# Seven instead of six quads of weights prepared in the fourth block, 3.3 chunks apart

## The chip, the cores and the metric

One core of a Trainium2 chip runs the whole program. The metric is the device time of one execution in microseconds. The kernel before took 774.9 us (median of three runs, 772.95 to 774.94).

## The reference

Attention with a band mask (four heads of 32 keys, four of every fourth key among 128), then two feed-forward layers on 2304 tokens of 512 features, all in float32; the weights are given as float64 words.

```python
x = attention(q, k, v)                     # (2304, 512)
h = x @ w_in; x = (h * cos(h)) @ w_out     # first feed-forward, width 2048
h = max(max(x @ w1, x @ w2), x @ w3)       # second feed-forward, width 768
out = h @ w_out2
```

## The kernel before

**Precision.** Every float32 operand of the large products is split into a high half (a cast) and a low half (the operand less its high half), and a product is three TensorE passes: high by high, low by high, high by low. So each operand costs one cast (ScalarE, VectorE or GpSimd) and one subtraction (VectorE or GpSimd).

**Stages.** Tokens of the first feed-forward go in five blocks: four of 512 and one of 256 tokens. A block is 16 steps, one for each 128 columns of the inner width; steps are numbered through, so the fourth block is steps 48 to 63 and the fifth 64 to 79. A step `s` has eight chunks of three matmuls: four of the first layer for step `s` (line 452, 512 or 256 columns), and four of the second layer for step `s - 3` (line 551). Between the two lie the argument reduction (`ff1_reduce`, lines 519 to 531), the sine on ScalarE (line 534), the product (line 540), its high half (line 541, which is recorded as line 214 on ScalarE and line 210 on GpSimd, in turn in the fourth block) and its low half (line 542). The halves `gt` have two buffers, so the high half of step `s` waits until TensorE has finished the second layer of step `s - 2`, at the end of step `s + 1`. Attention of later blocks runs beside the steps; its last pair is in the fourth block.

**The second feed-forward's weights.** They are multiplied by a seven-product scheme for 2 by 2 quarters. The weights come in nine quads of 2 by 2 quarter blocks; each quad needs four sums of quarters and the high and low halves of seven operands. The quads lie in DRAM as `wd`, and the finished halves are kept in DRAM as `opd`.

- Quads in `PRE` (2 to 7) are prepared in the fourth block: `pre_load` (line 708) loads the quad's two raw tiles `rawp`, from a pool of three buffers that the attention's `e` tiles use too; `pre_part` (line 714) makes one of four pieces. Pieces 0 and 1 are two sums (line 729, VectorE), a cast (line 735, ScalarE) and a subtraction (line 736, VectorE); pieces 2 and 3 a cast and a subtraction on GpSimd. Each piece takes its tiles from the five buffers of tag `qkv`, and stores its two halves to `opd` (line 740). The code writes a quad over two steps, one piece at chunks 2 and 6 of each, beginning at step 51; the next quad's load follows piece 3.
- Quads 0, 1 and 8 are prepared later: `raw_load` (line 644), `a_sums` (line 654, sums on line 667) and `a_part` (line 671, a cast on ScalarE, line 638, and a subtraction on GpSimd, line 639), with `a_keep` (line 701) to store them. `ff2_early` (line 975) does this for quads 0 and 1 in the fifth block, beside the making of the second layer's inputs from `x1raw` (`b_load`, line 800, five buffers of tag `qkv`; `b_make`, line 807).
- For every other quad, and for all of them in the second and third pass over tokens, `a_part` loads `wa` from `opd` (line 693).

**What sets the order.** TensorE's instructions are kept in the order of the code. From the fourth block on the order of the other engines and of SyncE's queue is chosen by the tile framework: the place in the code is a preference, an instruction can be put earlier or later, and each engine then works in the chosen order and waits at an instruction whose inputs aren't there.

```python
made = q < NQUAD and q not in PRE          # a_part, line 675
...
x = a1 if n == 2 else a22                  # pre_part, line 731
hl = [place(name, F32R)[:, :cols] for name in ("hi", "lo")]
nc.scalar.copy(hl[0], x)
(nc.vector if n < 2 else nc.gpsimd).tensor_tensor(
    out=hl[1], in0=x, in1=hl[0].bitcast(F32), op=ALU.subtract)
```

Of the kernel before, what the change touches and what calls it, by code (L numbers as in the profile page):

```python
# [30 lines left out]
NF1 = FF1 // 128  # L31
# [9 lines left out]
NB2 = NT // (2 * HALF)  # L41
NQUAD = 3 * NF2 // 2
LAG = 3
PRE = range(2, 8)
RUNS = 5
KEYS = 2 * QB + WIN
WSLOTS = 2 * NF1
# [117 lines left out]
def body(  # L165
# [381 lines left out]
    def acc_chunk(t0, first, last, w, gt, dm, copied=True):  # L547
        n_tok = gt.shape[-1]
        a_dm = acc[dm][:, :n_tok]
        for n, (a, x) in enumerate(PASSES):  # L550
            pe(nc.tensor.matmul(  # L551
                a_dm,
                w[:, a, 128 * dm : 128 * dm + 128],
                gt[:, x, :],
                start=first and n == 0,
                stop=last and n == 2,
            ))
        if last and copied:
            acc_copy(t0, n_tok, dm, "V" if dm % 2 else "A")
# [19 lines left out]
    def raw_exponent(n):  # L579
        if 0 <= n < len(halves2):  # L580
            exponent(pieces2[n])
# [47 lines left out]
    def slot_tile(n, shape, dt, name):  # L629
        return wp.tile(shape, dt, tag=f"w{n}", name=name)  # L630
# [13 lines left out]
    def raw_load(q):  # L644
        if q < NQUAD and q not in PRE:
            raws[q] = slot_tile(q % 3, [128, 2, 512], F32, "raw")
            nc.sync.dma_start(out=raws[q], in_=wd[q])
# [6 lines left out]
    def a_sums(q, n):  # L654
        if q < NQUAD and q not in PRE:
            r = raws[q]
            a11, a12, a21, a22 = (r[:, i, 256 * k : 256 * k + 256] for i in range(2) for k in range(2))
            if n == 0:
                if q < 2:
                    sums[q] = slot_tile(9, [128, 4, 256], F32, "ws")  # L660
                else:
                    sums[q] = gp.tile([128, 4, 256], F32, tag="g", name="ws")
                do = ((0, a21, a22, ALU.add), (1, sums[q][:, 0], a11, ALU.subtract))
            else:
                do = ((2, a11, a21, ALU.subtract), (3, a12, sums[q][:, 1], ALU.subtract))
            for k, x, y, op in do:
                nc.vector.tensor_tensor(out=sums[q][:, k], in0=x, in1=y, op=op)
# [3 lines left out]
    def a_part(q, n):  # L671
        if q >= NB2 * NQUAD:
            return
        cols = 256 * len(PARTS[n])
        made = q < NQUAD and q not in PRE
        dt = F32R if made else F32
# [21 lines left out]
    def kept_at(q, n):  # L698
        return opd[q, :, 2 * n : 2 * n + len(PARTS[n])].rearrange("p a n -> p (a n)").rearrange("p (a n) -> p a n", a=2)
# [8 lines left out]
    def pre_load(q):  # L708
        if q in PRE:
            raw_pre[q] = [sp.tile([128, 512], F32, tag="e", name="rawp") for _ in range(2)]  # L710
            for i in range(2):
                nc.sync.dma_start(out=raw_pre[q][i], in_=wd[q, :, i])

    def pre_part(q, n):
        if q not in PRE:
            return
        a1, a2 = raw_pre[q]
        a11, a12, a21, a22 = (r[:, 256 * k : 256 * k + 256] for r in (a1, a2) for k in range(2))
        place = lambda name, dt: ip.tile([128, 512], dt, tag="qkv", name=name)
        if n < 2:  # L720
            x = place("ws", F32)
            x1, x2 = x[:, :256], x[:, 256:]
            if n == 0:
                raw_pre["s2"] = x2
                do = ((x1, a21, a22, ALU.add), (x2, x1, a11, ALU.subtract))
            else:
                do = ((x1, a11, a21, ALU.subtract), (x2, a12, raw_pre.pop("s2"), ALU.subtract))
            for out, i0, i1, op in do:
                nc.vector.tensor_tensor(out=out, in0=i0, in1=i1, op=op)
        else:  # L730
            x = a1 if n == 2 else a22
        cols = x.shape[-1]
        part = (1, 2, 0, 3)[n]
# [3 lines that stand above are left out]
            out=hl[1], in0=x, in1=hl[0].bitcast(F32), op=ALU.subtract  # L737
        )
        for k in range(2):
            nc.sync.dma_start(out=kept_at(q, part)[:, k], in_=hl[k].bitcast(F32))  # L740
# [333 lines left out]
    def weight_loads(n, upto):  # L1074
        for _ in range(n):
            if at[0] < upto:
                w_load(order[at[0]], src[order[at[0]]])
                at[0] += 1
# [39 lines left out]
    def h_of(s):  # L1118
        t, f = divmod(s, NF1)
        if t < NBT - 1:  # L1120
            hv = (bank[6] if s == 2 else h_bank[(s + (s > 2)) % 2])[:, : BLOCKS[t]]
        else:
            hv = bank[4 + (s + 2) % 4][:, : BLOCKS[t]]
        return hv, h_chunks(hv, halves[("in", f)], STARTS[t] % RING, BLOCKS[t])
# [4 lines left out]
    n = len(first)  # L1129
# [172 lines left out]

    in_order = {e.engine for e in (nc.tensor, nc.vector, nc.scalar, nc.gpsimd)}
    NS = NBT * NF1
    PRE_AT = NS - 2 * NF1 + 3
    for s in range(NS + LAG):
        phase[0] = 1 if s < NF1 else 2 if s < NS - NF1 else 3
        assert s % NF1 or finished >= set(sum(plan[: s // NF1 + 1], []))
        if s == 0:
            weight_loads(WSLOTS, WSLOTS)  # L1310
        if s == PINNED:
            fixed.append(len(nc.cur_bb.bb.instructions))
        chunks = []
        if s < NS:
            hv, hc = hs[s] = hs[s] if s in hs else h_of(s)
            chunks += [("h", n, c) for n, c in enumerate(H_ORDER) if n >= begun.get(s, 0)]
        if s >= LAG:
            chunks += [("a", dm, 0) for dm in range(NC)]
        if NF1 <= s < PINNED:

            def chunk1(kind, x, c):
                if kind == "h":
                    hc(x, c)
                else:
                    t0, f0 = divmod(s - LAG, NF1)
                    last = f0 == NF1 - 1
                    acc_chunk(STARTS[t0], f0 == 0, last, halves[("out", f0)], g[s - LAG], x, False)
                    if last:
                        acc_done.append((STARTS[t0], BLOCKS[t0], x))

            step1(s, [lambda c=c: chunk1(*c) for c in chunks])
            chunks = []
            pairs = [x for x in pairs if x[2] not in pairs1[: next_of.get("W", 0)]]
            continue
        events = []
        if s == NF1:
            events += [(0, lambda: ff1_high(s - 2)), (0, lambda: ff1_low(s - 2))]
        if s < NF1:

            def chunk(kind, x, c):  # L1340
                if kind == "h":
                    hc(x, c)
                else:
                    f0 = s - LAG
                    acc_chunk(0, f0 == 0, False, halves[("out", f0)], g[f0], x)

            step0(s, [lambda c=c: chunk(*c) for c in chunks])
            raw_bits(s - NF1)
            chunks = []
        for j, (kind, x, c) in enumerate(chunks):  # L1350
            upto = j if j + 1 < len(chunks) else 7
            if kind == "h":
                hc(x, c)
                if x == NC - 1 and s >= NF1:
                    ff1_reduce(s, hv)
            else:
                t0, f0 = divmod(s - LAG, NF1)
                acc_chunk(STARTS[t0], f0 == 0, f0 == NF1 - 1, halves[("out", f0)], g[s - LAG], x)
            while events and events[0][0] <= upto and not (pairs and pairs[0][0] <= 8 * s + min(events[0][0], upto)):
                events.pop(0)[1]()  # L1360
            while pairs and pairs[0][0] <= 8 * s + upto:
                att_pair(*pairs.pop(0)[1:])
                while events and events[0][0] <= upto and not (pairs and pairs[0][0] <= 8 * s + min(events[0][0], upto)):
                    events.pop(0)[1]()
            if j == 1 and s >= NF1:
                if s - 1 < NS:
                    ff1_g(s - 1)
            q, n = divmod(s - PRE_AT, 2)
            q += PRE.start
            if s == PRE_AT - 1 and j == 6:  # L1370
                pre_load(q + 1)
            if s >= PRE_AT and q in PRE and j in (2, 6):
                pre_part(q, 2 * n + j // 6)
                if n and j == 6:
                    pre_load(q + 1)
            if j == 1:
                raw_exponent(s - NF1)
            if j == 5:
                raw_bits(s - NF1)
        k = s - (NS - NF1)  # L1380
        if k >= -1:
            ff2_early(k)
# [94 lines left out]
```

## Time and profile before

| | us |
|---|---|
| median of three runs | 774.9 |
| lowest, highest | 772.95, 774.94 |
| the profiled execution | 773.13 |
| its span, first to last instruction | 771.4 |
| TensorE matmul busy | 760.3 (99%) |
| VectorE busy | 567.7 (74%) |
| ScalarE busy | 445.2 (58%) |
| GpSimd busy | 102.3 (13%) |

A busy share is an average over the whole span. The profile has further views: windows (busy time of each engine in a stretch), the timeline of one engine (start, duration, and in brackets the idle time before an instruction and what ended it), and the DMA issues with the time from issue to landing.

### The profile page before, as it was taken

The page shows a single profiled execution, that of the slowest core. Times are in us where ns is not written, and L with a number is a line of the kernel's source. Part 1 is how long each engine was busy: PE and PEld are TensorE (multiplying, and loading weights), DVE is VectorE, ACT ScalarE, POOL GpSimd, SP SyncE. Part 2 cuts the span into 40 slices and gives each one's busy share as a digit, 9 for nine tenths or more (in the row PEclk, how much of TensorE's full clock was granted, in tenths as well). Part 3 has the DMA queues.
Part 4 walks back from the last instruction along what each step waited for, and adds up shares of the span by engine and source line. Part 5 has one row for each costly group of instructions (what it writes and reads, how often), then busy time and mean ns, then how long its engine had stood idle before and what let it go on. Part 6 is the DMA issues. An engine that isn't in the chain of part 4 may idle for free.

```text
span 771.4 us, 13658 instructions
## 1 busy us (share of the span) xinstructions
PE 760.3 (99%) x4760; PEld 672.7 (87%) x4760; DVE 567.7 (74%) x1497; ACT 445.2 (58%) x1080; POOL 102.3 (13%) x107
## 2 busy tenths in 40 slices
PE   9999999999999999999999999999999999999997
PEld 7777777878878878887888899899999999999997
DVE  6999999777776788877866769996675666646742
ACT  7889999779573777764544435554434333433330
POOL 2422121302022202010112203100200000000000
PEclk9999999999999999999999999999999999999999
DMA  9983111243434443433456563398765888467802
GB/s 355 416 315 143 37 43 67 85 165 105 125 119 138 129 157 125 131 100 110 165 191 218 188 206 134 112 300 277 244 198 186 243 253 258 136 190 243 255 22 83
DMA packets 60405, 134.32 MB, mean 174 GB/s; under 512 B 6704, under 2 KB 21168, under 8 KB 60336
## 3 DMA queue, kind: packets, MB, share of 16 engines
q1 hardware_dynamic: 60336, 133.44, 51.7%
q8 instruction: 38, 0.62, 0.3%
q14 instruction: 31, 0.25, 0.1%
HBM read 101.17 MB, written 32.24 MB: 173 GB/s over the span
## 4 chain that ended last, share of the span: by engine, by line
PE 79%; DVE 10%; ACT 6%; DMA 3%; issue 1%; POOL 0%; ACTq 0%; DVEq 0%; SPq 0%
PE bank L826 25%; PE bank L551 19%; PE bank L452 19%; PE bank L944 9%; PE bank L341 2%; ACT e L291 2%; PE bank L410 2%; PE bank L393 1%; DMA wod<-wh 1%; PE bank L321 1%; ACT L291 1%; DVE ring L639 1%; DVE wx L263 1%; ACT r L291 1%; DMA wh<-in_w_o 1%
## 5 line engine op out<-in xcount | busy, mean ns | idle before, releaser
L452 PE MATMUL bank<-ring,w 128*128 128x512 f32 (+1 forms) x960 | 219.1, 374 | 1.5 <-DVE ring L434 1.5
L551 PE MATMUL bank<-gt,w 128*128 128x512 f32 (+1 forms) x960 | 215.8, 371 | 1.5 <-DVE gt L542 1.3
L826 PE MATMUL bank<-ring,wa 128*128 128x384 f32 x1134 | 198.0, 334 | 0.0
L826 PEld LDWEIGHTS bank<-ring,wa 128*128 128x128 f32 x1134 | 196.6, 188 | 0.0
L551 PEld LDWEIGHTS bank<-gt,w 128*128 128x128 f32 x960 | 166.6, 189 | 33.1 <-DVE gt L542 1.8
L452 PEld LDWEIGHTS bank<-ring,w 128*128 128x128 f32 x960 | 165.4, 189 | 34.0 <-DVE ring L434 1.9
L291 ACT ACTIVATE r<-r,hpi 128x512 f32<-128x512 f32 (+1 forms) x80 | 54.6, 683 | 54.2 <-DVE r L531 35.0
L291 ACT ACTIVATE e<-e,m 96x128 f32<-96x128 f32 x192 | 75.0, 393 | 5.8 <-DVE m L351 5.5
L842 ACT COPY s<-bank 128x384 f32<-128x384 f32 x54 | 26.0, 481 | 45.5 <-PE bank L826 45.4
L291 ACT ACT_TABLE_LOAD x38 | 48.8, 1283 | 1.7 <-PEq L1463 0.7
L351 DVE CUSTOM_DVE_ANT_0 e<-bank,cs 96x128 f32<-96x128 f32 x192 | 42.7, 282 | 9.1 <-PE bank L341 9.1
L860 DVE TENSOR_TENSOR s<-s,bank 128x384 f32<-128x384 f32 x36 | 19.9, 553 | 37.9 <-PE bank L826 37.9
L944 PE MATMUL bank<-whole,w 128*128 128x384 f32 x252 | 47.5, 334 | 0.0
L944 PEld LDWEIGHTS bank<-whole,w 128*128 128x128 f32 x252 | 44.0, 188 | 0.0
L210 POOL TENSOR_SCALAR gt<-r 128x512 fp32r<-128x512 f32 x27 | 18.9, 700 | 178.3 <-PE bank L551 120.0
L282 POOL TENSOR_TENSOR w<-wx,w 128x512 fp32r<-128x512 f32 x20 | 26.3, 1318 | 80.5 <-DVE w L214 46.5
L291 ACT ACTIVATION_READ_ACCUMULATOR e<-e,m 96x1 f32 x192 | 36.5, 190 | 0.0
L255 ACT ACTIVATE wh<-wh 128x256 f32<-128x256 f32 x48 | 20.6, 436 | 27.0 <-DMA wh<-in_w 19.2
L488 DVE CUSTOM_DVE_ANT_0 r<-bank,r 128x512 f32<-128x512 f32 x39 | 26.8, 687 | 12.8 <-ACT r L466 12.8
L496 DVE TENSOR_TENSOR r<-bank,r 128x512 f32<-128x512 f32 x47 | 32.2, 685 | 3.3 <-ACT r L291 3.1
L790 ACT CAST whole<-mx 128x384 fp32r<-128x384 f32 x36 | 18.6, 516 | 27.1 <-DVE mx L862 14.6
L385 DVE TENSOR_TENSOR e<-e,z 96x512 f32<-96x512 f32 x47 | 32.0, 710 | 0.9
(106 smaller groups left out, 992.2 us busy)
## 6 DMA issues: line engine op xcount, KB each, us to landing
wa<-opd SPq DMA_DIRECT2D x72, 512.0 KB, 4.6
qkv<-in_qkv SPq DMA_DIRECT2D x48, 336.0 KB, 4.0
wh<-in_w SPq DMA_DIRECT2D x36, 256.0 KB, 2.9
w<-in_w_in SPq DMA_DIRECT2D x16, 512.0 KB, 8.7
w<-in_w_out SPq DMA_DIRECT2D x16, 512.0 KB, 9.4
wa<-opd SPq DMA_DIRECT2D x24, 256.0 KB, 4.2
wd<-wh SPq DMA_DIRECT2D x36, 128.0 KB, 1.8
opd<-hi SPq DMA_DIRECT2D x18, 256.0 KB, 2.0
```

What stands on the lines that cost most here:

```text
L255: nc.scalar.activation(high, high, AF.Prelu, scale=2.0**-112, alpha=2.0**32)
L282: eng.tensor_tensor(out=w[:, 1, :], in0=words.pop(key), in1=w[:, 0, :].bitcast(F32), op=ALU.subtract)
L291: last_table.append(nc.scalar.activation(*args, **kw).ins)
L351: nc.vector.tensor_tensor_reduce(out=e[:, 2 * j + h, :], in0=places_of[j, h], in1=mask[:, kind, :], scale=-1.0 / math.sqrt(D), scalar=3e38 ...
L385: eng.tensor_tensor(out=e, in0=e, in1=z[:, n, :].unsqueeze(2).to_broadcast([QB, 4, KB]), op=ALU.mult)
L452: pe(nc.tensor.matmul(hv, w[:, a, 128 * c : 128 * c + 128], ring[c][:, x, c0 : c0 + n_tok], start=n == 0 and j == 0, stop=n == NC - 1 and ...
L488: nc.vector._custom_dve(dve_ops.TENSOR_ADD_SAT, out=r, in0=hv, in1=r, s0=ARG_HI, s1=ARG_LO)
L496: nc.vector.tensor_tensor(out=r, in0=hv, in1=r, op=ALU.mult)
L551: pe(nc.tensor.matmul(a_dm, w[:, a, 128 * dm : 128 * dm + 128], gt[:, x, :], start=first and n == 0, stop=last and n == 2,))
L826: nc.tensor.matmul(out, ops[q][a][:, x, 128 * c : 128 * c + 128], b_op(b, c)[:, y], start=first and c == 0 and n == 0, stop=c == 1 and n == 2,
L842: nc.scalar.copy(x, bank_of(q)[to][:, :HALF])
L944: nc.tensor.matmul(to, w[p][:, 128 * at : 128 * at + 128], x[y], start=first and k == 0 and j == 0, stop=k == len(steps) - 1 and j == 2, s ...
```

## The change

`PRE` becomes quads 1 to 7, so quad 1 is prepared in the fourth block, and the fifth loads its finished halves from `opd`. The places of the pieces are no longer chunks 2 and 6 of each step: piece `n` of the 28 stands `24 + round(3.3 n)` chunks after the beginning of the fourth block, that is from chunk 0 of step 51 to chunk 1 of step 62. The first load stands four chunks ahead of the first piece, at chunk 4 of step 50 in place of chunk 6.

```diff
-PRE = range(2, 8)
+PRE = range(1, 8)
+PRE_SLOTS = [24 + round(3.3 * n) for n in range(28)]
...
-    PRE_AT = NS - 2 * NF1 + 3
+    pre_slots = [8 * (NS - 2 * NF1) + n for n in PRE_SLOTS]
...
-            q, n = divmod(s - PRE_AT, 2)
-            q += PRE.start
-            if s == PRE_AT - 1 and j == 6:
-                pre_load(q + 1)
-            if s >= PRE_AT and q in PRE and j in (2, 6):
-                pre_part(q, 2 * n + j // 6)
-                if n and j == 6:
-                    pre_load(q + 1)
+            if 8 * s + j == pre_slots[0] - 4:
+                pre_load(PRE.start)
+            if 8 * s + j in pre_slots:
+                q, n = divmod(pre_slots.index(8 * s + j), 4)
+                pre_part(PRE.start + q, n)
+                if n == 3:
+                    pre_load(PRE.start + q + 1)
```

## Rows read from the trace of the kernel before

**Rows 1.** The page's busy times (share of the span, instructions).

```profile
PE 760.3 (99%) x4760; PEld 672.7 (87%) x4760; DVE 567.7 (74%) x1497; ACT 445.2 (58%) x1080; POOL 102.3 (13%) x107
```

**Rows 2.** Timeline of TensorE, fourth and fifth block: start, duration, what, idle before.

```profile
374.03 3.01 PE L452 MATMUL bank<-ring,w 128*128 128x512 f32 x12
...
442.40 2.88 PE L551 MATMUL bank<-gt,w 128*128 128x512 f32 x12
...
446.56 2.91 PE L551 MATMUL bank<-gt,w 128*128 128x512 f32 x12
...
450.74 2.91 PE L551 MATMUL bank<-gt,w 128*128 128x512 f32 x12
...
454.92 2.91 PE L551 MATMUL bank<-gt,w 128*128 128x512 f32 x12
...
495.85 1.84 PE L551 MATMUL bank<-gt,w 128*128 128x256 f32 x12 [0.36 <-DVE gt L542]
498.61 1.44 PE L551 MATMUL bank<-gt,w 128*128 128x256 f32 x10 [0.92 <-DVE gt L542]
500.31 1.92 PE L551 MATMUL bank<-gt,w 128*128 128x256 f32 x12 [0.26 <-ACT gt L214]
502.06 18.19 PE L826 MATMUL bank<-ring,wa 128*128 128x384 f32 x104
```

**Rows 3.** Windows: length, PE, PEld, DVE, ACT, POOL busy, clock, DMA share, GB/s.

```profile
395.90:406.80 10.90, 10.90 (x49) 9.01 (x48) 7.39 (x14) 5.12 (x9) 2.14 (x4) 1.00 0.59 210
...
475.00:483.60 8.60, 8.60 (x74) 8.60 (x74) 8.60 (x22) 5.21 (x12) 3.40 (x4) 1.00 0.37 147
```

**Rows 4.** Timeline of VectorE in the fourth block.

```profile
376.86 0.42 DVE L729 TENSOR_TENSOR ws<-rawp 128x256 f32<-128x256 f32 x1
...
400.51 0.43 DVE L729 TENSOR_TENSOR ws<-rawp 128x256 f32<-128x256 f32 x1 [2.86 <-issue]
...
401.31 0.68 DVE L526 CUSTOM_DVE_ANT_0 r<-bank,r 128x512 f32<-128x512 f32 x1
402.08 0.76 DVE L736 TENSOR_TENSOR lo<-ws,hi 128x512 fp32r<-128x512 f32 x1
...
404.63 0.68 DVE L736 TENSOR_TENSOR lo<-ws,hi 128x512 fp32r<-128x512 f32 x1
...
412.31 0.43 DVE L729 TENSOR_TENSOR ws<-rawp 128x256 f32<-128x256 f32 x1 [3.11 <-issue]
...
435.92 0.42 DVE L729 TENSOR_TENSOR ws<-rawp 128x256 f32<-128x256 f32 x1 [2.80 <-DMA rawp<-wd]
...
439.37 0.69 DVE L542 TENSOR_TENSOR gt<-r,gt 128x512 fp32r<-128x512 f32 x1
...
443.87 0.68 DVE L542 TENSOR_TENSOR gt<-r,gt 128x512 fp32r<-128x512 f32 x1
```

**Rows 5.** Timelines of GpSimd and of SyncE's queue between quads 4 and 5.

```profile
405.53 2.17 POOL L736 TENSOR_TENSOR lo<-rawp,hi 128x512 fp32r<-128x512 f32 x2 [3.23 <-ACT hi L735]
...
408.43 0.99 SPq L712 DMA_DIRECT2D rawp<-wd  x2
```

**Rows 6.** DMA issues, 374 to 450 us: count, size, median us from issue to landing.

```profile
rawp<-wd SPq DMA_DIRECT2D x9, 256.0 KB, 3.5
```

**Rows 7.** The page's DMA issues: loads of finished halves.

```profile
wa<-opd SPq DMA_DIRECT2D x72, 512.0 KB, 4.6
```

**Rows 8.** Timelines of VectorE, GpSimd and SyncE in the fifth block.

```profile
470.63 0.56 DVE L639 TENSOR_TENSOR ring<-x1raw,ring 128x384 fp32r<-128x384 f32 x1
...
477.08 1.32 DVE L542 TENSOR_TENSOR gt<-r,gt 128x256 fp32r<-128x256 f32 x1
...
480.46 0.42 DVE L667 TENSOR_TENSOR ws<-ws,raw 128x256 f32<-128x256 f32 x1
...
476.82 1.30 POOL L639 TENSOR_TENSOR wa<-raw,wa 128x512 fp32r<-128x512 f32 x1 [1.70 <-ACT wa L638]
...
443.60 2.32 SPq L804 DMA_DIRECT2D x1raw<-x1d  x5
```

## The prediction

> **What bounds the kernel now.** I read the page's busy times first. TensorE is busy for 760.3 us, 99% of the span of 771.4 us [rows 1], and the granted clock is 1.00, the 2.4 GHz level, in the windows of both blocks [rows 3]. So a change pays only where TensorE waits, and costs only where it makes TensorE wait. Next I read TensorE's own timeline through the two blocks that the diff touches [rows 2]. The reader should see three things there. From 374.03 us (first-layer matmuls of step 51) to 442.40 us (second-layer matmuls of step 63, half a step after its start) lie 12.5 steps of 5.47 us, no idle time noted, a chunk of three matmuls taking 0.68 us. At the end of the fifth block TensorE waits three times, 0.36, 0.92 and 0.26 us, all for the halves of `g`: 1.54 us together. From 502.06 us it runs on. **1.54 us, 0.2% of the time, is all that the touched stages can give back.**
>
> Then the windows by engine [rows 3]: in 475.0 to 483.6 us VectorE is busy for all 8.60 us, so there it is VectorE that falls behind and later makes TensorE wait. In 395.9 to 406.8 us, in the fourth block, it is busy for 7.39 of 10.90 us. That is the room into which the change moves work.
>
> Last, VectorE's order in the fourth block [rows 4]. The first sum of quad 2 starts at 376.86 us, that of quad 4 at 400.51, of quad 5 at 412.31, of quad 7 at 435.92: (435.92 - 376.86) / 5 = 11.81 us a quad, where the code asks for two steps, 10.94 us. Each quad starts 0.87 us later against TensorE than the one before it. The timeline puts 3.11 us of VectorE idle time ahead of 412.31. **The six quads already run as a chain of waits, not at their written places.**
>
> **The chain of one quad.** From the first sum at 400.51 to the second low half's end, 404.63 + 0.68 = 405.31 us, VectorE works without a pause, with operations of the first feed-forward between; four sums of 0.43 and two low halves of 0.68 to 0.76 us are 3.1 us of it [rows 4]. GpSimd's two low halves follow, 405.53 + 2.17 = 407.70 us [rows 5]. Behind the last store, SyncE starts the next raw loads at 408.43 us, two in 0.99 us [rows 5]. Such a load lands 3.5 us after issue in the median [rows 6], and the next quad starts at 412.31. So 4.8 us for VectorE, 2.4 for GpSimd, 0.7 for SyncE, 3.9 for the loads: 11.8 us. Nothing in the diff shortens the last three. Only the operations between can change, since the places in the code decide what is preferred. These places bind only loosely: the low half at 402.08 us stands after the clip at 401.31, though the code writes it ahead [rows 4].
>
> The Trainium skill (DMA: Bandwidth & Descriptors, Anatomy of one DMA) fits a transfer, there one that GpSimd starts, as about 2.0 us plus its bytes at 436 GB/s; I estimate 2.6 us from it for 256 KB, which would take 0.9 us off the chain and nearly close the drift of 0.87. The trace has 3.5 us, so the row holds here.
>
> **The change part by part.**
>
> Quad 1 leaves the fifth block. Four sums go there, each moving the next VectorE operation by 0.34 us (480.46 to the next one's start in the same dense stretch; take its own 0.42 us as the upper end) [rows 8]: 1.4 to 1.7 us. Its four GpSimd subtractions leave too. While one runs, at 476.82 us, a VectorE subtraction of the 256-column kind takes 1.32 instead of some 0.42 us [rows 8]; 0 to 0.9 us each, I take 0.4, four times: 1.6 us. ScalarE's four copies leave, on an engine with room. So VectorE gets about 3 us back (1.4 to 5.3), ahead of waits of 1.54 us that it causes. I book the full **-1.54 us**; the ends are 0 (the backlog of the seventh quad, below, eats it) and -1.54, since there is no more to take.
>
> In their place quad 1's operands are loaded: three loads of 512 KB and one of 256 KB, a further 1.8 MB, less the raw load of 512 KB that now goes to the fourth block. A 512 KB load takes 4.6 us from issue to landing [rows 7], and the DMA engines are 37% busy in 475.0 to 483.6 us [rows 3]. They are written three steps and more ahead of 502.06, and the operands are first used behind it. Cost 0; if a slot came free too late, one landing, 4.6 us, on the first use at 502.06 us or behind.
>
> The fourth block gets a quad: four sums, two low halves on VectorE, four copies on ScalarE, two low halves on GpSimd, two loads and eight stores on SyncE. As busy time it is hidden: VectorE has 10.90 - 7.39 = 3.51 us free in two steps [rows 3]. What counts is the chain: seven links of 11.8 us in place of six. Behind a waiting sum, VectorE's queue holds the products and low halves of `g`, and TensorE waits for those. The low half at 439.37 us ends at 440.05; TensorE uses it in step 63 at 442.40: a slack of 2.35 us. The next, 443.87 + 0.68 = 444.55 us, is used at 446.56: 2.0 us [rows 2, 4].
>
> Quad 1 can't start much ahead of where quad 2 starts now, for its second raw tile takes a buffer of the last attention pair in either kernel, so the seventh quad takes a link more: its sum at 435.92 + 11.81 = 447.7 us, the low half behind it done at 440.05 + 11.81 = 451.9. It is needed at 450.74, as a step of the fifth block is shorter: **1.1 us late**. The one after that, 444.55 + 11.81 = 456.4 us, is needed at 454.92, pushed to 456.0 by then: **0.3 us more** [rows 2, 4]. So +1.4 us at the seam. Below, the bound is 0: 1.4 us less of chain, two chunks' earlier start, and it's gone. Above, case C.
>
> SyncE's loads of the fifth block's inputs start at 443.60 us now, because their five buffers come free there [rows 8]. With seven quads they come a link later, 455.4 us, and land in some 4 us; the first split made of them starts at 470.63 [rows 8]. Cost 0, with 11 us of cover.
>
> Spacing 3.3 in place of 4 chunks: 13.2 chunks a quad, 9.0 us by the code. The chain needs 11.8, so pieces are late wherever they are written. I take 0 for it, the ends -1.4 us (sums get ahead of first-layer work, the chain shortens) and case C's price.
>
> The sum: -1.54 + 1.4 = -0.1 us with the chain as it is, -1.5 if it tightens by a quarter of a microsecond a link. I take -0.4. The profiled execution took 773.13 us, 1.7 over its span, and 1.8 below the median of 774.9 of the three runs shown; they range from 772.95 to 774.94, so either is usual. From the middle, 774.0: **773.6 us**. A measurement can tell about 0.3%, 2.3 us, from no change.
>
> **The rivals.**
>
> A, the forecast: the seventh quad hangs over the seam, costs what the end of the fifth block gives back, -0.4 us: 772.7 us from the profiled execution, 774.5 from the median. Chance 0.46.
>
> B: the pieces, written earlier, are preferred over first-layer work and a link falls below 11.6 us. No wait at the seam, all of 1.54 us is gained: 771.6 from the profiled execution, 773.4 from the median. For it: 1.7 us of the 4.8 that a link spends on VectorE aren't the quad's own work [rows 4]. Against: the other 7.0 us of a link are untouched. Chance 0.24; still within 0.3%, as a rule.
>
> C, the one that makes it slower: VectorE's queue follows the written places, 9.0 us a quad, while loads still come at 11.8. Place: quad 7's first sum is written at step 60, chunk 7, on TensorE's clock 374.03 + 9 x 5.47 + 4.8 = 428.1 us; the chain brings it at 376.86 - 1.4 + 6 x 11.81 = 446.3. Behind it stand step 60's product and halves, 2.7 us by operations of 0.43 to 0.76 us, with the two sums ahead, done at 449.0, needed at 442.40 [rows 2, 4]: TensorE waits for 6.6 us. Less 1.54: +5.1, 778.2 us from the profiled execution, 780.0 from the median. It decides from a link of 10.7 us (6 x 10.7 = 64.2 in place of 70.9). For it: the six quads now all start at the same place of the code, ahead of the same clip. Against: that they start late by now, and still don't hold TensorE up. Chance 0.21.
>
> D: more is gained than the profile shows, as executions at 774.9 us may hold longer waits of just these kinds, up to 1.8 us, that the change removes as well: 771.4 us or less, -0.45%. Chance 0.06. E: the quad is made early but something else of the fifth block's end stays late, or quad 1 isn't read from the early result: no change, 774.0. Chance 0.03.
>
> **How the numbers follow.** Slower by over 0.3%: most of C, 0.18, and 0.03 of A: 0.21. Faster by over 0.3%: D and a little of B, 0.08. Within: 0.71. The range reaches from B's and D's lower end, 771.3, into C, to 778.2.
>
> **What would show it.** Right: seven starts of quads 11 to 12 us apart in VectorE's timeline, the last near 447 us; new TensorE waits of about a microsecond at 446 to 456 us for low halves of `g`; no such waits at 495 to 501 us; TensorE dense behind. B: starts under 11.6 us apart, no wait at the seam. C: several microseconds of TensorE waits between 430 and 450 us with VectorE waiting for raw loads. The forecast is wrong if TensorE's idle time in the two blocks changes by more than 2.3 us either way, or if time moves behind 502 us.

## The result and the profile after

The changed kernel takes 779.09 us (median of four runs, 778.46 to 779.33) beside 774.31 us before (772.95 to 774.94): ratio 1.0054, 95% interval 1.0029 to 1.0079. The medians differ by 4.8 us, and the time lies just beyond the upper end of the range forecast (778.2). The profiled execution has a span of 777.3 us, 5.9 over that of before.

The page's busy times, to be set beside [rows 1]: TensorE is busy 3.1 us longer for the same 4760 matmuls, and its span grows by 5.9.

```profile
PE 763.4 (98%) x4760; PEld 673.4 (87%) x4760; DVE 567.2 (73%) x1499; ACT 443.5 (57%) x1080; POOL 99.6 (13%) x105
```

TensorE's timeline, the lines that answer to [rows 2] and those with idle time (start, duration, what, idle before and what ended it):

```profile
374.01 3.01 PE L453 MATMUL bank<-ring,w 128*128 128x512 f32 x12
...
441.68 3.02 PE L453 MATMUL bank<-ring,w 128*128 128x512 f32 x12 [1.86 <-DVE r L541]
...
447.26 1.60 PE L453 MATMUL bank<-ring,w 128*128 128x256 f32 x12
...
461.57 1.33 PE L552 MATMUL bank<-gt,w 128*128 128x256 f32 x9 [0.18 <-ACT o L565]
463.55 0.62 PE L552 MATMUL bank<-gt,w 128*128 128x256 f32 x3 [0.64 <-DVE o L565]
464.00 1.59 PE L453 MATMUL bank<-ring,w 128*128 128x256 f32 x12
...
469.46 1.45 PE L552 MATMUL bank<-gt,w 128*128 128x256 f32 x10 [0.75 <-DVE gt L543]
...
501.62 1.83 PE L552 MATMUL bank<-gt,w 128*128 128x256 f32 x12 [0.34 <-DVE gt L543]
504.38 1.45 PE L552 MATMUL bank<-gt,w 128*128 128x256 f32 x10 [0.93 <-DVE gt L543]
506.08 1.91 PE L552 MATMUL bank<-gt,w 128*128 128x256 f32 x12 [0.25 <-ACT gt L215]
507.82 2.42 PE L827 MATMUL bank<-ring,wa 128*128 128x384 f32 x13
```

Both traces have step 51's first layer at 374.0 us. From there to the first matmul of the second feed-forward it is 128.03 us before [rows 2] and 507.82 - 374.01 = 133.81 here: **5.78 of the 5.9 us lie in this stretch.** Three pieces make it up. Step 64 begins at 447.26, 73.25 us in, where before it was 71.09 (445.12 in its timeline): +2.16, with the wait of 1.86 us at 441.68. Step 68 begins at 464.00, 89.99 us in, where before it was 86.51 (460.54): another +1.32, with the waits for output copies. The other +2.30 comes behind that, a wait of 0.75 us and short gaps up to some 487 us. And the three waits at the end, which were to be gained, are still there: 1.52 us.

VectorE's timeline: the chain's sixth and seventh start, the product that TensorE waits for at 441.68, and a standstill that was not in the kernel before.

```profile
375.97 0.42 DVE L730 TENSOR_TENSOR ws<-rawp 128x256 f32<-128x256 f32 x1
...
438.09 0.42 DVE L730 TENSOR_TENSOR ws<-rawp 128x256 f32<-128x256 f32 x1 [4.42 <-DMA rawp<-wd]
...
440.94 0.68 DVE L541 TENSOR_TENSOR r<-bank,r 128x512 f32<-128x512 f32 x1
...
448.62 0.43 DVE L730 TENSOR_TENSOR ws<-rawp 128x256 f32<-128x256 f32 x1 [1.92 <-POOL gt L211]
...
468.01 0.42 DVE L520 TENSOR_SCALAR kk<-bank 128x256 int32<-128x256 f32 x1 [4.52 <-DMA x1d<-o]
```

The seven quads start 12.1 us apart ((448.62 - 375.97) / 6), the last at 448.62 us. What it does is seen in SyncE's queue, and in the DMA issues of 455 to 470 us (count, size, median us to landing):

```profile
455.84 0.85 SPq L741 DMA_DIRECT2D opd<-lo  x1
458.19 2.87 SPq L805 DMA_DIRECT2D x1raw<-x1d  x5
461.10 0.43 SPq L648 DMA_DIRECT2D raw<-wd  x1
461.57 2.77 SPq L568 DMA_DIRECT2D x1d<-o  x4
```

```profile
x1d<-o SPq DMA_DIRECT2D x4, 256.0 KB, 6.4
```

The loads `x1raw` start at 458.19 us, not at 443.60 [rows 8], since their five buffers are the seventh quad's. So they, and the raw tile of quad 0, now go out directly ahead of the four stores of the fourth block's outputs. Before, the same four stores landed in 2.1 us:

```profile
x1d<-o SPq DMA_DIRECT2D x4, 256.0 KB, 2.1
```

Now they take 6.4. The windows of the changed kernel (length, PE, PEld, DVE, ACT, POOL busy, clock, DMA share, GB/s) show the DMA engines busy at 0.88 to 0.97 from 458 to 468 us:

```profile
458.00:460.00 2.00, 2.00 (x11) 1.68 (x10) 1.40 (x4) 0.81 (x2) 0.00 (x0) 1.00 0.97 292
...
464.00:466.00 2.00, 2.00 (x19) 2.00 (x18) 0.00 (x0) 0.41 (x1) 0.00 (x0) 1.00 0.88 282
466.00:468.00 2.00, 2.00 (x19) 2.00 (x18) 0.00 (x0) 0.00 (x0) 0.00 (x0) 1.00 0.95 369
```

An output tile `o` (line 564) is one of the five tiles of tag `r`, in which VectorE also reduces its arguments. Until a store has landed there is none free: VectorE does nothing from 464 to 468 us.

### The profile page after: what moved, and what is told of

The parts are those of the page before. It is cut to its first block, busy times and chain, and to the rows that moved or that the text cites. A ratio compares the mean times of both kernels' runs of the same rounds, so it can differ in the third digit from the quotient of the medians.

```text
span 777.3 us, 13685 instructions
## 1 busy us (share of the span) xinstructions
PE 763.4 (98%) x4760; PEld 673.4 (87%) x4760; DVE 567.2 (73%) x1499; ACT 443.5 (57%) x1080; POOL 99.6 (13%) x105
## 4 chain that ended last, share of the span: by engine, by line
PE 77%; DVE 10%; DMA 5%; ACT 5%; issue 1%; SPq 1%; POOL 1%; POOLq 0%; DVEq 0%; ACTq 0%
PE bank L827 25%; PE bank L453 19%; PE bank L552 18%; PE bank L945 9%; PE bank L342 2%; PE bank L411 2%; PE bank L394 2%; ACT r L292 1%; DMA w<-in_w_in 1%; DMA w<-in_w_out 1%; ACT e L292 1%; DMA rawp<-wd 1%; DMA x1d<-o 1%; DVE r L532 1%; DVE r L529 1%
```

## The experiments

The stretch above, from step 51's first layer to the second feed-forward, is given for every profile; it leaves out the attention ahead, whose length moves by a microsecond or more between executions. Runs were made in groups, each with the kernel before measured beside it: e1 to e4, e5 to e8, e9 to e11, and e12. The ratio is to that one. Medians of different groups can't be compared closely, as the kernel before itself has 773.28 in one and 774.77 in another.

| run | stretch, us | median, us | before beside it, us | ratio to before (95%) |
|---|---|---|---|---|
| before | 128.03 | 774.31 | |  |
| changed | 133.81 | 779.09 | 774.31 | 1.0054 (1.0029 to 1.0079) |
| e1: six quads, 3.3 apart | 127.78 | 773.66 | 773.28 | 0.9997 (0.9987 to 1.0008) |
| e2: seven, 4 apart | 133.84 | 778.75 | 773.28 | 1.0063 (1.0044 to 1.0083) |
| e3: changed, input loads behind the stores | 128.39 | 774.98 | 773.28 | 1.0016 (1.0004 to 1.0027) |
| e4: before, quad 1 not prepared | 125.80 | 771.81 | 773.28 | 0.9975 (0.9966 to 0.9984) |
| e5: changed, fourth raw buffer | 126.32 | 772.95 | 774.51 | 0.9985 (0.9968 to 1.0002) |
| e6: six quads, fourth raw buffer | 127.80 | 775.88 | 774.51 | 1.0014 (1.0000 to 1.0028) |
| e7: e5 and e3 together | 125.78 | 772.62 | 774.51 | 0.9976 (0.9957 to 0.9996) |
| e8: before, with e3's order | 128.51 | 774.72 | 774.51 | 1.0001 (0.9987 to 1.0015) |
| e9: changed, again | 132.95 | 780.02 | 774.09 | 1.0084 (1.0061 to 1.0107) |
| e10: e3 again | 129.04 | 774.80 | 774.09 | 1.0006 (0.9991 to 1.0020) |
| e11: e7 again | 126.39 | 772.30 | 774.09 | 0.9982 (0.9970 to 0.9993) |
| e12: before, six small attention buffers | 127.76 | 775.07 | 774.77 | 1.0000 (0.9982 to 1.0018) |

**The number of quads, or the spacing?** `e1_six_33` and `e2_seven_40` take one half of the diff each.

```diff
-PRE = range(1, 8)
-PRE_SLOTS = [24 + round(3.3 * n) for n in range(28)]
+PRE = range(2, 8)                                        # e1
+PRE_SLOTS = [24 + round(3.3 * n) for n in range(24)]
...
+PRE_SLOTS = [24 + 4 * n for n in range(28)]              # e2, PRE as changed
```

> Six quads (2 to 7) as before, but 3.3 chunks apart. Theory (the seventh link of the chain costs, the spacing does nothing): the chain runs at 11.8 us a quad whatever the spacing, so the time is that of before, 774.3 us within 1.5, and TensorE's wait ahead of step 63's first layer stays at 0.3 us or less. Rival (the closer spacing makes pieces stand ahead of first-layer work): 776.5 us or more, with a new TensorE wait between 430 and 445 us.

> Seven quads (1 to 7) 4 chunks apart. Theory (the seventh link costs): as the changed kernel, 779 us within 1.5, with the wait of 1.9 us ahead of step 63's first layer and VectorE's wait of 4.5 us for the stores of the block's outputs. Rival (spacing): 776 us or less.

Both went as the theory said. With seven quads the spacing does not even change the order: with 4 chunks and with 3.3 the framework puts the same instructions in the same order on all five queues. With six, the first sum comes 0.9 us earlier against step 51, and the time stays. **The places written in the code have no effect on the time; the seventh quad is the whole change.**

**The queue of loads ahead of the stores.** `e3_late_xload` makes the first input loads wait, in SyncE's queue, for the output stores.

```diff
-        nc.sync.dma_start(out=x1d[dm, :, t0 : t0 + n_tok], in_=o)
+        stored.append(nc.sync.dma_start(out=x1d[dm, :, t0 : t0 + n_tok], in_=o))
...
+            with tc.issue_after(stored[-1].ins) if t == c == 0 else nullcontext():
                 nc.sync.dma_start(out=x, in_=x1d[2 * k + c, :, t0 : t0 + HALF])
...
-        if k in (1, 8):
+        if k in (3, 8):
```

> The changed kernel, with the fifth block's input loads put behind the four stores of the fourth block's outputs in SyncE's queue. Theory (these loads wait for the seventh quad's buffers and hold up the stores behind them, and so VectorE and TensorE): VectorE's wait of 4.5 us at 463 to 468 us falls under 1 us, TensorE's waits between 461 and 486 us, 3.5 us in all, go almost wholly, the wait of 1.9 us ahead of step 63 stays: 3.0 to 3.6 us under the changed kernel, 775.5 to 776.5 us. Rival (VectorE simply has too much to do behind the seam): less than 1 us under the changed kernel, 778 us or more.

It gave 3.8 us back beside e2, the seven-quad kernel of its group, and its repeat e10 gave 5.2 beside e9: more than expected. SyncE's queue and VectorE's timeline of this kernel:

```profile
455.88 0.40 SPq L650 DMA_DIRECT2D raw<-wd  x1
...
460.54 2.30 SPq L570 DMA_DIRECT2D x1d<-o  x4
462.89 2.36 SPq L808 DMA_DIRECT2D x1raw<-x1d  x5
```

```profile
462.96 0.42 DVE L520 TENSOR_SCALAR kk<-bank 128x256 int32<-128x256 f32 x1 [0.48 <-DMA x1d<-o]
```

The stores land in 2.5 us, the standstill of 4.52 us is 0.48, and of the three waits at the end only one of 0.24 us is left (two, of 0.52 and 0.24 us, in e10). Quad 0's raw tile, too, goes out earlier here, at 455.88 in place of 461.10 us; how the harm divides between it and the five input loads is not shown. The wait ahead of step 63 came out at 0.32 us here, which was not expected. `e8_six_late`, the same order in the kernel before, is the control.

> The kernel before, with the fifth block's input loads behind the output stores in SyncE's queue. Theory: in the kernel before these loads found their buffers free in time (first one issued at 443.6 us), so the order does nothing: within 0.5 us of before. Rival: a gain of 1 us or more, so that what the third run gained wasn't the seventh quad's delay.

No difference (1.0001): with six quads these loads are long done. So what e3 gives back is harm of the seventh quad.

**Does the wait ahead of step 63 move by itself?** The edit of e3 touches nothing ahead of it. `e9_after_again` and `e10_late_again` are the two kernels once more.

> The changed kernel once more, for a second profile (a comment line added). What it tells: whether the wait ahead of step 63's first layer (1.86 us in the changed kernel, 1.70 with 4 chunks, 0.32 in the third run, though nothing ahead of it differs there) moves from execution to execution with the raw loads. If it does: anything from 0.3 to 2 us, and VectorE's wait for the output stores 4 to 5 us again, 778 to 780 us. If the queue order of the third run shortened it by some way: 1.6 us or more again.

> The third run's kernel once more, for a second profile. Theory (chain and wait move with the raw loads): a wait ahead of step 63 of 0.3 to 2 us, no wait over 1 us of VectorE for the output stores, 774 to 776.5 us. Rival (the queue order shortens the wait at step 63): 0.4 us or less again.

It does. In the changed kernel it is now 0.73 us, in e3's 0.78:

```profile
440.21 3.02 PE L454 MATMUL bank<-ring,w 128*128 128x512 f32 x12 [0.73 <-DVE r L542]
```

The kernel of `e8_six_late`, with six quads, has it too, though the kernel before has not:

```profile
440.14 3.02 PE L452 MATMUL bank<-ring,w 128*128 128x512 f32 x12 [0.45 <-DVE r L540]
```

In six-quad and seven-quad kernels alike, VectorE's order has the sixth quad's first sum, which waits for its raw tiles, ahead of the product that TensorE needs. When that sum starts, counted from step 51's first layer, decides the wait:

| run | sixth quad's first sum, us | wait ahead of step 63, us |
|---|---|---|
| changed | 64.08 | 1.86 |
| e2 | 63.74 | 1.70 |
| e10 | 62.76 | 0.78 |
| e9 | 62.71 | 0.73 |
| e8 (six quads) | 62.44 | 0.45 |
| e3 | 62.30 | 0.32 |
| before (six quads) | 61.89 | none |
| e4 (six quads) | 61.44 | none |
| e12 (six quads) | 61.12 | none |
| e1 (six quads) | 60.55 | none |

So the wait costs 0.3 to 1.9 us by execution. It is about what the first sum of the quad that is sixth in turn is later than 62.0 us, and stands ahead of the seventh quad. The sum comes later with seven quads, 63.1 us in the mean against 61.5 with six, though the first quad starts 0.9 us earlier; why is not taken apart. The waits behind 464 us came again in e9 (1.20 us at 468.49 us, behind a standstill of VectorE of 4.99 us); e10 has none between 462 and 498 us.

**The gain alone.** `e4_no_quad1` has no quad 1 in the fifth block and none in the fourth. `raw_load` and `a_sums` get the same condition as `made` below.

```diff
-        made = q < NQUAD and q not in PRE
+        made = q < NQUAD and q not in PRE and q != 1
...
     def kept_at(q, n):
+        q = 2 if q == 1 else q
```

> The kernel before, with quad 1 not prepared at all: no sums, casts, subtractions, stores or raw load for it; the fifth block loads quad 2's halves in its place, so one third of two of the six pairs of inner columns is computed with other weights. It is the gain of the change without its cost. The prediction's term (VectorE's backlog causes the waits of 1.54 us at the end of the fifth block): these waits go, 1.2 to 1.8 us under before. Rival (these waits are the latency from the last first-layer product to its second-layer use, whatever VectorE had to do earlier): the three waits stay at 1.4 to 1.6 us, the time within 0.5 us of before.

The term of the prediction stands: 128.03 - 125.80 = 2.2 us in the stretch, a ratio of 0.9975, and TensorE runs through the last steps with one wait of 0.18 us:

```profile
493.83 4.48 PE L551 MATMUL bank<-gt,w 128*128 128x256 f32 x36
498.49 1.92 PE L551 MATMUL bank<-gt,w 128*128 128x256 f32 x12 [0.18 <-ACT gt L214]
500.25 2.07 PE L827 MATMUL bank<-ring,wa 128*128 128x384 f32 x11
```

The gain is more than the 1.54 us of noted waits. Of the same 48 matmuls, the kernel before has the first 14 here and the rest in [rows 2]:

```profile
493.66 1.84 PE L551 MATMUL bank<-gt,w 128*128 128x256 f32 x14
```

They take 502.06 - 493.66 = 8.40 us there and 500.25 - 493.83 = 6.42 us here. The idle time that the view notes leaves out 0.6 of these 2.0 us.

**The chain itself.** A fourth raw buffer lets each quad's raw tiles come a quad ahead. The mask tile of the attention, free after its last pair, is the buffer.

```diff
-    smp = pool("smp", 8)
+    smp = pool("smp", 6)
...
-    cs = csp.tile([128, 3 * KB + QB], F32, name="cs")
+    cs = csp.tile([128, 512], F32, tag="cs", name="cs")[:, : 3 * KB + QB]
...
-            raw_pre[q] = [sp.tile([128, 512], F32, tag="e", name="rawp") for _ in range(2)]
+            raw_pre[q] = [
+                csp.tile([128, 512], F32, tag="cs", name="rawp") if i and (q - PRE.start) % 2
+                else sp.tile([128, 512], F32, tag="e", name="rawp")
+                for i in range(2)
+            ]
...
                 pre_load(PRE.start)
+                pre_load(PRE.start + 1)
...
-                    pre_load(PRE.start + q + 1)
+                    pre_load(PRE.start + q + 2)
```

> The changed kernel with a fourth buffer for the raw tiles (the attention's mask tile, free after its last pair) and each quad's raw tiles loaded a quad earlier; two of eight small attention buffers go to make room. Theory (a link of 11.8 us is the wait of a quad for its raw tiles behind the last subtraction of the one before): 3 to 4 us of each link go, it takes 8 to 10 us, the seventh quad starts before 440 us, the wait ahead of step 63 and VectorE's wait for the output stores both go, and the gain of 1.5 to 1.9 us is kept: 771 to 772.5 us. Rival (the link is set by the casts, subtractions and stores through five shared buffers): links of 11 us or more, 776 us or more.

> The kernel before (six quads, 4 chunks apart), with the same fourth buffer and the raw tiles loaded a quad earlier. Theory: its chain gets shorter too, but it held TensorE up nowhere, so the time is that of before within 0.7 us, 772.6 to 774.0. Rival (the six-quad chain cost something unseen): 1.5 us or more under before.

> Seven quads with the fourth raw buffer, and the fifth block's input loads behind the output stores in SyncE's queue. Theory: with the chain shortened these loads no longer wait for buffers, so the order in the queue does nothing: within 0.5 us of the kernel with the fourth buffer alone. Rival (the order also frees VectorE in the fifth block): 1 us or more under it.

The chain falls to 8.7 us a quad. The first, second and last start in e7:

```profile
376.04 0.41 DVE L736 TENSOR_TENSOR ws<-rawp 128x256 f32<-128x256 f32 x1
384.85 0.41 DVE L736 TENSOR_TENSOR ws<-rawp 128x256 f32<-128x256 f32 x1
...
428.04 0.41 DVE L736 TENSOR_TENSOR ws<-rawp 128x256 f32<-128x256 f32 x1
```

(428.04 - 376.04) / 6 = 8.67 us, and the seventh quad starts 20 us earlier than in the changed kernel. e5 and e7 have no wait over 0.25 us in the stretch, and it takes 126.3 and 125.8 us. e5's median of 772.95 us is somewhat above the 771 to 772.5 expected, and its interval just reaches 1.0002. e6 was expected within 0.7 us of before and its median is 1.4 us above, a ratio of 1.0014 at the edge of its interval; its stretch is no longer than before. That e7's order adds something over e5 is not shown: the intervals overlap.

> The seventh run's kernel once more, to firm its interval against before. Theory: 1.5 to 2.3 us under before, ratio 0.997 to 0.998; rival: no different from before, within 1 us.

> The kernel before with six instead of eight small attention buffers, the control for the kernels with the fourth raw buffer, whose first 374 us took up to 2.6 us longer in three of their four profiles. If the smaller pool costs that: 1 us or more over before, step 51 beginning at 375.3 us or later. If not: within 0.5 us of before, step 51 at 374.0 to 375 us.

The repeat of e7 came to 0.9982 (0.9970 to 0.9993): **seven quads with the chain shortened beat the kernel before, by 1.4 to 1.9 us by the two ratios, and so the changed one too.** The control with six small buffers gave 1.0000 (0.9982 to 1.0018), so no cost of these buffers is seen, and the longer first 374 us in some profiles of the fourth-buffer kernels is left unexplained.

## Why the prediction was wrong

- **What bounds, and the chain.** Right in the main. TensorE's waits decide, and the chain runs by itself: seven starts 12.1 us apart (forecast 11.8), the last at 448.62 us (forecast 447.7). That the last start fits so well is in part luck: the first quad starts 0.9 us earlier than taken, the next five links take 12.4 us in the mean and the last 10.5. That spacing costs or gives nothing was taken at 0 and is 0 (e1, e2).
- **The gain, -1.54 us.** The cause holds, and there was more to take than the noted waits (2.2 us in e4's stretch); the condition did not hold: it needs a VectorE that isn't held up elsewhere. In the changed kernel the standstill of 4.52 us, more than the 3 us that the change frees, brought the three waits back; with e3's order 0.24 and 0.76 us of them are left (e3, e10).
- **The seam, +1.4 us for late low halves.** The kind was right (work of VectorE late behind a waiting sum), the place was not. The first limit is not the low half's use three steps later but the product `hv * sin`: it reads the bank of step 61, into which step 63's first layer writes, as there are two banks for it (`h_bank`). The prediction read a slack of 2.35 us from the low half at 439.37 [rows 4]. The line of VectorE just ahead of it in the kernel before shows none, for its product ends at 439.46, and TensorE's next first layer, step 63's, starts at 439.51:

```profile
438.77 0.69 DVE L540 TENSOR_TENSOR r<-bank,r 128x512 f32<-128x512 f32 x1
```

```profile
439.51 3.06 PE L452 MATMUL bank<-ring,w 128*128 128x512 f32 x12
```

  The wait measured 0.3 to 1.9 us, and it stands behind the sixth quad. The low halves that were to cost 1.1 and 0.3 us behind the seventh cost nothing: in e3 the first of them ends at 451.07 + 0.68 = 451.75 us (forecast 451.9), TensorE begins the matmuls that use it at 451.48, and no idle time is noted. The copies of the outputs, which the sum left out, are late by the overhang (1.32 us of the stretch in the changed kernel). e3 has the seam without the loads: 0.32 + 0.54 + 0.64 = 1.5 us of waits, against 1.3 gained at the end; e10 has 1.6 against 0.8. So the forecast's sum of -0.1 comes out at +0.4 and +1.0 us in the stretch (e3, e10), its size of the seam by luck.
- **The step that failed: "SyncE's loads ... Cost 0, with 11 us of cover".** It asked who waits for these loads (nobody, for 11 us) and not what they delay on their way. A link later, they leave ahead of the output stores; 1.5 MB of loads has been issued in the 3.4 us ahead of the stores, and these land in 6.4 us for 2.1. Their tiles are VectorE's scratch tiles, so VectorE stands still for 4.52 us, and TensorE waits behind it. Price: 133.81 and 132.95 us (changed, e9) against 128.39 and 129.04 (e3, e10), some 4.7 us of the stretch. Of these 0.75 are the wait ahead of step 63, which the order doesn't touch; without it the stretches are 131.95 and 132.22 against 128.07 and 128.26, and **the term put at 0 cost 3.9 us**.
- **The rivals.** B's price came true once the chain was shortened (e7, e11). C had the sign right. The wait of 1.86 us at 441.68 is of its kind: VectorE stands idle for raw tiles with a product of the first layer behind them. But the order of the sixth quad's pieces against that product is the one before had, the wait is 1.9 and not 6.6 us, and 3.6 of the 5.8 us lie behind the start of step 64. Its chance, 0.21, stood in the main for the wrong mechanism. E named the end of the block staying late: it did, by the loads, but the price was not E's "no change". D is not seen.
- The Trainium skill's fit (DMA: Bandwidth & Descriptors, Anatomy of one DMA) is for one transfer that GpSimd starts; the estimate from it for 256 KB is 2.6 us. The traces, with stores from SyncE's queue, agree roughly when little is ahead (2.1 us before, 2.5 and 3.0 in e3 and e10) and not when 1.5 MB is (6.4 us). The same section says that the DMA engines work through their queues without waiting on semaphores, which fits stores that queue up behind loads issued earlier.

## What to carry to other kernels

A transfer that is moved later has two costs: who waits for it, and what it then stands in front of. The second must be read from the queue and the landing times of whatever is issued just behind, and from whose buffers those transfers hold. A series of pieces that runs late against its written places is a chain of waits; adding one more pays only after the chain has been shortened (here one more buffer, 12.1 to 8.7 us a link). And an operation's slack is the smallest over all that its result releases, the bank that it frees included.

## What the runs showed of the hardware

The landing of a 256 KB store moved from 2.1 to 6.4 us with what had been issued in the 3.4 us ahead of it, at a DMA share of 0.88 to 0.97. The wait ahead of step 63 moved between 0.32 and 1.86 us over five profiles of kernels with the same instructions ahead of it, as the sixth quad's first sum came 62.3 to 64.1 us behind step 51; VectorE's idle time ahead of that sum is ended by the landing of its raw tiles (4.42 us in the changed kernel).
